# A state-space block and its MLP on one core: token rows as pairs of 64-column matmuls, a table set loaded in another place, and a new order of the front

## The chip, the core and the metric

The kernel runs on one core of a Trainium2 chip. The metric is the device time of one execution in microseconds, the median over three runs. A core has five engines that run side by side and wait for each other by semaphores: PE (TensorE, matrix multiply, with PEld for its weight loads), DVE (VectorE), ACT (ScalarE), POOL (GpSimd) and SP, which here only issues transfers (DMA).

## The reference

The inputs are one sequence of 2048 tokens with 512 channels, in bf16. Two layers follow each other, both with a residual: a long convolution whose kernel is made from a diagonal state-space model (128 states for each channel), and an MLP of width 1376.

```python
dt = exp(log_dt)[:, None]
P = exp((dt * (A_re + 1j * A_im))[:, :, None] * arange(L))
K = einsum("dn,dnl,dn->dl", C, P, dt * B).real          # 512 x 2048
y = irfft(rfft(pad(u)) * rfft(pad(K)))[:L] + u * Dskip   # u = layernorm(x)
h = x + y
h2 = h + gelu(layernorm(layernorm(h)) @ w1 + b1) @ w2 + b2
```

## The kernel before

The convolution is done with a Fourier transform of length 4096 that is split into two stages of matmuls, so that a token number falls into a partition and a row: the view `xv` of the input, `(p j) d -> p j d` with `j` of 16, puts token 16 p + j on partition p as row j.

The front (everything up to the MLP) runs in these stages, which overlap:

- `prefix` makes small constants on POOL and DVE: `bits` and `pf` hold pieces of the partition number, `mask` says which of eight columns belongs to a partition, `cols` and `bw` hold factors and phases.
- `first_stage` makes from them `BD`, the matrix of the first stage of the transform, and `D` (in the profile `Dm`), its transpose, which at the end turns frequencies into token rows. Both have two halves h of 128 columns. In each half a column is zero unless its q, the partition number's last three bits, has the parity h, so half the columns of `D[:, h]` are zero.
- `params` computes the step (`step`, the exponential of `log_dt`), then `th` and the phases `psi`, `psw` and `five`; `exps` computes exponentials of `th` into `Pt` and `Q` on ACT; `p_half` and `q_half` multiply them by sines (`pv`, `qv`, `s`, `sq`); `kgen` makes samples of K with small matmuls (`kps`), writes them to DRAM (`KD`) and reads them back in another layout (`kt`). This is done twice, for channels 0 to 255 (half 0) and 256 to 511 (half 1).
- `norm_in` normalises the tokens (`st`, `rs`, `u`), multiplies them by `BD` (`aps`), and sends the result through DRAM (`A_dram`) into `X`. `x_stage` does the second stage (`xps`).
- `conv` makes the spectrum of K from `kt` (`kfps`, then `kf`), multiplies it with `X` (`pa`, `pb`), transforms back (`zps`, then `z`), and sends z through DRAM (`Zd`) into `ZT`, where the contraction index lies on the partitions. When X has been read, `residual` loads the tokens into it again; its first two calls come in the front, on POOL and SP, the last two in `late_loads`.
- Token rows: `early_rows` (tiles y0, half 0 of rows 0 to 7) and `head_rows` (tile yh, half 1 of rows 0 to 3) add the residual with a matmul by the identity and add `D[:, 0]` and `D[:, 1]` times `ZT` into the same PSUM tile. In the MLP `y_rows` (tile y1, half 1 of rows 4 to 7) and `y_row` (tile y2, a full row of 512) do the same, without the identity. The profile writes y0, y1 and y2 all as y: L1113 and L1115 are those of `half_rows`, L1224 is `y_row`.

The MLP (`mlp`) runs over four blocks of four rows: `up` makes `h1ps` (4 matmuls for each of 11 pieces of the hidden width) with a GELU on ACT, `down` makes `o2ps` (11 matmuls for each row), and DVE adds the residual h and SP writes the row out. `y_row` of the next block stands between the `up` steps of the present one, two matmuls at a time after each second step.

What sets the order: every piece of the front is an `S.op` with a number. The list `ORDER` holds 4 x number + choice, in the order in which the pieces are emitted, and so in which they stand in each engine's queue; the choice picks the engine where a piece may run on either of two. Each engine takes its queue strictly in this order. The dependencies written in `S.op` (such as `x0`, the list of the back transforms, in the calls that make `r0`) are what the search for the order had to keep. The MLP stands in the order of the code.

The activation tables of ACT are loaded when a function of another set comes: the helper `logs` loads the set for logarithm and exponential if the last marked set is not this one, `sines` marks the other. In `step` the exponential of `log_dt` stands without `logs`.

Of the kernel before, what the change touches and what calls it, by code (L numbers as in the profile page):

```python
# [16 lines left out]
P = 128  # L17
# [64 lines left out]
def bc(ap, shape):  # L82
    return ap.to_broadcast(shape)

# [35 lines left out]
def stt(nc, out, a, s, b, o1, o2):  # L120
    nc.vector.scalar_tensor_tensor(out, a, s, b, o1, o2)
# [67 lines left out]
def prefix(nc0, S, K, cp, ct, c2):  # L189
# [41 lines left out]
    split = ((3, 15), (0, 7), (0, 1), (1, 1))  # L231
    bits = c2.tile([P, 4], i32, name="bits")
    for n, (sh, m) in enumerate(split):
        ts(nc, bits[:, n:n + 1], pi[:], sh, ALU.logical_shift_right, m, ALU.bitwise_and)
    pf = ct.tile([P, 4], f32, name="pf")
    nc.vector.tensor_copy(pf[:], bits[:])
    t1, q, odd, b1 = (pf[:, n:n + 1] for n in range(4))
# [9 lines left out]
    t1s = col(t1, 1.0 / 64, 0.0)  # L247
# [12 lines left out]
    ts(nc, mask[:], kf[:, 0:8], q, ALU.is_equal)  # L260
# [222 lines left out]
def params(nc, S, K, cp, pp, sc, cv, psp, raws, ldt, dtb, grb):  # L483
    T, S2, Z = {}, S.op, {}

    def step():
        for h in range(2):
            d = slice(HW * h, HW * h + HW)
            nc.scalar.activation(dtb[:, d].rearrange("p (j g) -> p g j", g=4), ldt[:, d].rearrange("p (g j) -> p g j", g=4), ACT.Exp)
# [530 lines left out]
def head_rows(nc, S, K, psp, cv, o_tail):  # L1020
    K.o_head = []
    for n in range(2):
        cell = {}

        def main(cell=cell, n=n):
            cell["y"] = psp.tile([P, 2, 512], f32, name="yh", tag="p", bufs=PB)
            for r in range(2):
                o, j = cell["y"][:, r, 0:HW], 2 * n + r
                nc.tensor.matmul(o, lhsT=K.ident[:], rhs=K.X[:, j, 1, 0:HW], start=True, stop=False)
                for h in range(2):  # L1030
                    nc.tensor.matmul(o, lhsT=K.D[0:96, h], rhs=K.ZT[0:96, 1, h, j, :], start=False, stop=False)
# [23 lines left out]
        m = S.op("PE", 0.65, main, K.o_z[0:6] + K.o_r0[0:1] + [o_tail], acq="p")  # L1055
# [54 lines left out]
def half_rows(nc, K, out, hh, js, more=False):  # L1110
    for j in range(js.start, js.stop):
        if more:
            nc.tensor.matmul(out[:, j - js.start], lhsT=K.ident[:], rhs=K.X[:, j, hh, 0:HW], start=True, stop=False)  # L1113
        for h in range(2):
            nc.tensor.matmul(out[:, j - js.start], lhsT=K.D[:, h], rhs=K.ZT[:, hh, h, j, :], start=(h == 0 and not more), stop=(h == 1))  # L1115
# [16 lines left out]
def early_rows(nc, S, K, psp, z0, r0):  # L1132
    for n in range(2):
        cell = {}
        js = slice(4 * n, 4 * n + 4)

        def mm(cell=cell, js=js):
            cell["y"] = psp.tile([P, 4, HW], f32, name="y0", tag="p", bufs=PB)
            half_rows(nc, K, cell["y"], 0, js, True)

        def keep(cell=cell, js=js):
            nc.scalar.copy(K.h[:, js, 0:HW], cell["y"][:])

        def stats(cell=cell, js=js):
            for j in range(js.start, js.stop):
                nc.vector.bn_stats(K.st[:, j, 0, :], cell["y"][:, j - js.start])

        m = S.op("PE", 1.35, mm, z0 + r0[n:n + 1], acq="p")
        s = S.op("DVE", 1.5, stats, [m], rel=[m])
        k = S.op("ACT", 1.0, keep, [m], rel=[m])  # L1150
        K.o_early.append(S.op("NONE", 0.0, lambda: None, [s, k]))
# [38 lines left out]
def residual(q, K, xv, n):  # L1190
    q.dma_start(K.X[:, 4 * n:4 * n + 4, :, 0:HW], xv[:, 4 * n:4 * n + 4].rearrange("p j (h d) -> p j h d", h=2))


def mlp(nc, tc, K, w1, w2, b2, xv, ov):
    with tc.tile_pool(name="m_sb", bufs=1) as sb, tc.tile_pool(name="m_rot", bufs=2) as rot, tc.tile_pool(name="m_ps", bufs=2, space=PSUM) as ps1:
# [25 lines left out]
        def y_row(tb, jj):  # L1221
            yp = yps[tb, jj] = ps1.tile([P, 1, 2, HW], f32, name="y2", tag="yps")
            for h in range(2):
                nc.tensor.matmul(yp[:, 0], lhsT=K.D[:, h], rhs=K.ZT[:, :, h, 4 * tb + jj, :], start=(h == 0), stop=(h == 1))  # L1224
# [40 lines left out]
        def down(tb, jj):  # L1265
            j, h = 4 * tb + jj, hT[tb % 2]
            parts = 2 if tb == 3 and jj == 3 else 1
            for n in range(parts):
# [7 lines left out]
                nc.sync.dma_start(ov[j][:, d], ot[:])  # L1276
# [39 lines left out]
def kernel(ctx, tc, A_u, A_A_re, A_A_im, A_B_re, A_B_im, A_C_re, A_C_im, A_log_dt, A_Dskip,  # L1316
# [25 lines left out]
    xv = x_dram.rearrange("(p j) d -> p j d", j=16)  # L1342
# [14 lines left out]
    for n in range(4):  # L1357
        nc.sync.dma_start(x[:, 4 * n:4 * n + 4], xv[:, 4 * n:4 * n + 4])
# [56 lines left out]
    r0 = K.o_r0 = [S.op(("POOL", "SP"), (0.8, 0.45), lambda e, n=n: residual(nc.gpsimd if e == "POOL" else nc.sync, K, xv, n), x0[2 * n:2 * n + 2], lat=3.0) for n in range(2)]  # L1415
# [5 lines left out]
    mlp(nc, tc, K, B_w1, B_w2, B_b2, xv, out_dram.rearrange("(p j) d -> j p d", j=16))  # L1421
# [31 lines left out]
```

## Time and profile before

| what | us |
|---|---|
| three runs | 261.58, 263.01, 263.51 |
| median | 263.01 |
| span of the profiled execution | 260.3 |

The span goes from the first to the last instruction of one profiled execution on its only core; the whole time of that execution isn't listed beside it, so it is told here by the distance from the runs: the shortest is 1.3 above the span, the median 2.7. The transfers move 33.61 MB in all, a mean of 129 GB/s. The granted clock of TensorE was 1.000.

How to read the lines that follow: a row of the timeline has the start and the duration in us, the engine, the line of the code, the operation, output <- inputs, shapes, a count, and in brackets the idle time of the engine just ahead, with what ended it. A row of the chain of waits has start, duration and what. In a row of stretches, the stretch and its length come first, then the busy time of PE, PEld, DVE, ACT and POOL with instruction counts, the clock, and the share and rate of the DMA engines. Matmuls are pipelined: from start to start is what one costs in a stream, its own duration has a tail that lies beside the next. In the slices each digit is a tenth of busy share in a fortieth of the span.

### The profile page before, as it was taken

How to read it: one execution, taken by the hardware profiler on the slowest of the kernel's cores; microseconds unless marked ns; L12 is line 12 of the kernel's file. 1: busy time of each engine (PE TensorE's matmuls, PEld its weight loads, DVE VectorE, ACT ScalarE, POOL GpSimd, SP SyncE). 2: the span in 40 equal slices, each digit the busy share in tenths (PEclk: the TensorE clock that was granted, in tenths of full speed). 3: DMA queues.
4: the chain of work that ended last, by engine and by line, in shares of the span. 5: the costliest groups of instructions: out<-in, count | busy, mean ns of one | idle time of the engine just before them, and what ended most of it. 6: DMA issues, size and time to landing. Idle time of an engine off the chain costs nothing.

```text
span 260.3 us, 4481 instructions
## 1 busy us (share of the span) xinstructions
PE 220.3 (85%) x1585; PEld 138.3 (53%) x1585; DVE 203.3 (78%) x447; ACT 179.5 (69%) x303; POOL 40.0 (15%) x104
## 2 busy tenths in 40 slices
PE   2899308765688797899999999968999999999994
PEld 2323102322276585567988888857744444444443
DVE  6999999998999999999688999975836754761022
ACT  6999999999999999998833565448604703612810
POOL 8922960000003000100560010010000000000000
PEclk9999999999999999999999999999999999999999
DMA  5802951967695910410189678969541033022001
GB/s 166 293 7 34 191 162 61 162 170 244 183 357 148 227 11 24 139 44 0 53 180 267 185 201 242 264 197 240 141 102 59 1 63 101 0 54 80 31 26 54
DMA packets 49442, 33.61 MB, mean 129 GB/s; under 512 B 22154, under 2 KB 47900, under 8 KB 49164
## 3 DMA queue, kind: packets, MB, share of 16 engines
q1 hardware_dynamic: 47676, 28.66, 41.8%
q0 software_dynamic: 1744, 4.68, 7.1%
q8 instruction: 12, 0.20, 0.3%
q14 instruction: 10, 0.08, 0.1%
HBM read 18.65 MB, written 11.26 MB: 115 GB/s over the span
## 4 chain that ended last, share of the span: by engine, by line
PE 43%; DVE 16%; ACT 6%; DMA 6%; issue 2%; POOL 0%; DVEq 0%; POOLq 0%; ACTq 0%
PE o2ps L1273 14%; PE h1ps L1260 12%; PE kfps L930 8%; DVE Pt L79 5%; DMA ZT<-Zd 4%; DVE Q L79 3%; DVE X L79 2%; PE kps L765 2%; ACT Pt L673 2%; DVE pa L79 2%; DVE pb L79 2%; ACT sq L142 2%; DMA Zd<-z 2%; DVE X L91 1%; PE y L1224 1%
## 5 line engine op out<-in xcount | busy, mean ns | idle before, releaser
L1263 ACT ACTIVATE hT<-h1ps,b_sb 128x512 bf16<-128x512 f32 (+3 forms) x55 | 31.9, 604 | 41.9 <-PE h1ps L1260 40.2
L1260 PE MATMUL h1ps<-y2T,wide 128*128 128x512 bf16 (+3 forms) x220 | 40.5, 336 | 0.6 <-DVE ve L75 0.6
L1273 PE MATMUL o2ps<-w_sb,hT 128*128 128x512 bf16 (+3 forms) x187 | 38.7, 366 | 0.0
L930 PE MATMUL kfps<-kt,M 128*128 128x256 bf16 x320 | 37.9, 273 | 0.0
L79 DVE TENSOR_TENSOR ot<-o2ps,h 128x512 bf16<-128x512 f32 (+1 forms) x17 | 11.0, 658 | 30.3 <-PE o2ps L1273 16.9
L930 PEld LDWEIGHTS <-M 128*128 128x128 bf16 x320 | 31.3, 98 | 4.9 <-issue 1.2
L1260 PEld LDWEIGHTS <-wide 128*128 128x128 bf16 (+1 forms) x220 | 21.8, 100 | 17.0 <-issue 0.8
L1273 PEld LDWEIGHTS <-hT 128*128 128x128 bf16 (+1 forms) x187 | 18.3, 98 | 19.7
L79 DVE TENSOR_TENSOR Pt<-s,Pt 128x512 bf16<-128x512 bf16 (+1 forms) x48 | 23.0, 510 | 0.9 <-ACT s L142 0.3
L844 PE MATMUL aps<-u,BD 128*128 128x512 bf16 x32 | 10.2, 407 | 15.2 <-DVE u L839 11.2
L89 ACT CAST z<-zps 128x1024 bf16<-128x1024 f32 (+1 forms) x15 | 14.8, 992 | 10.6 <-PE zps L969 10.6
L673 ACT ACTIVATE Pt<-th 128x256 bf16<-128x256 f32 x64 | 20.7, 401 | 0.0
L142 ACT ACTIVATE sq<-qv 128x1024 bf16<-128x1024 int16 x20 | 20.1, 1077 | 0.0
L142 ACT ACTIVATE s<-pv 128x1024 bf16<-128x1024 int16 x16 | 16.9, 1077 | 0.0
L89 ACT CAST a<-aps 128x1024 bf16<-128x1024 f32 x16 | 15.8, 1053 | 0.5 <-DMA A_dram<-a 0.5
L738 PE MATMUL qv<-RQ,PQ 128*128 128x512 bf16 (+1 forms) x64 | 11.6, 298 | 4.7 <-ACT a L89 1.6
L844 PEld LDWEIGHTS <-BD 128*128 128x128 bf16 x32 | 3.0, 99 | 21.6 <-DVE u L839 14.3
L91 DVE CAST X<-xps 128x1024 bf16<-128x1024 f32 x12 | 14.3, 1219 | 0.0
L79 DVE TENSOR_TENSOR h<-y,X 128x512 f32<-128x512 f32 x10 | 6.9, 686 | 8.6 <-PE y L1224 5.6
L79 DVE TENSOR_TENSOR Q<-sq,Q 128x1024 bf16<-128x1024 bf16 x20 | 13.0, 685 | 0.1
L681 ACT ACTIVATE Q<-th 128x256 bf16<-128x256 f32 x40 | 13.0, 401 | 0.0
L449 POOL DMA_DIRECT2D Dp<-Dd x24 | 11.9, 504 | 7.2 <-DMA Dd<-ds 6.9
(246 smaller groups left out, 446.9 us busy)
## 6 DMA issues: line engine op xcount, KB each, us to landing
A_dram<-a SPq DMA_DIRECT2D x16, 256.0 KB, 2.6
X<-A_dram SPq DMA_DIRECT2D x4, 1024.0 KB, 7.2
Zd<-z SPq DMA_DIRECT2D x15, 256.0 KB, 3.4
x<-in_A_u_dram SPq DMA_DIRECT2D x4, 512.0 KB, 6.9
ZT<-Zd POOLq DMA_DIRECT2D x8, 256.0 KB, 4.1
ZT<-Zd SPq DMA_DIRECT2D x8, 256.0 KB, 3.6
out_dram<-ot SPq DMA_DIRECT2D x15, 128.0 KB, 1.9
X<-in_A_u_dram SPq DMA_DIRECT2D x3, 512.0 KB
```

The costliest lines, as they stand in the source:

```text
L79: (nc.vector if e == "DVE" else nc.gpsimd).tensor_tensor(out, a, b, op)
L89: nc.scalar.copy(out, in_)
L91: nc.vector.tensor_copy(out, in_)
L142: nc.scalar.activation(out, v.bitcast(i16)[..., 0:2 * n:2], ACT.Sin, scale=S2PI / 65536)
L449: nc.gpsimd.dma_start(t[o::128 // cnt], bass.AP(row.tensor, row.offset + 1024 * kh, [[0, cnt], [1, 1024]]))
L673: nc.scalar.activation(K.Pt[:, 1, :, k, :], K.th[:, ds].rearrange("p (e g) -> p e g", g=4), ACT.Exp, scale=float(8 * k))
L681: nc.scalar.activation(K.Q[:, 1, :, m, :], K.th[:, ds].rearrange("p (e g) -> p e g", g=4), ACT.Exp, scale=float(OFFS[m]))
L844: nc.tensor.matmul(ps[:, h, :], lhsT=K.BD[:, h].rearrange("p a b -> p (a b)"), rhs=cell["u"][:], start=True, stop=True)
L930: nc.tensor.matmul(ps[:, k, c, :], lhsT=K.M[:, t, k0 + k, c, :], rhs=kt[:, t, :], start=((plain or c == 1) and t == 0), stop=(t == 4))
L1260: nc.tensor.matmul(pt[:fs, 0:n], lhsT=K.w1_sb[:, dc, fc * P:fc * P + fs], rhs=(y2T[tb][:, dc, js, :] if tb or js.start else K.y2T[:, dc]). ...
L1263: nc.scalar.activation(hT[tb % 2][:fs, fc, cols], pt[:fs, 0:n], ACT.Gelu_apprx_tanh, bias=K.b1_sb[:fs, fc:fc + 1], scale=1.0)
L1273: nc.tensor.matmul(pt[:], lhsT=h[:fs, fc, jj * P:(jj + 1) * P], rhs=K.w2_sb[:fs, fc, d], start=(fc == 0), stop=(fc == NFC - 1))
```

## The change

Three things are changed.

The tokens are dealt in another way: the new view `dealt`, `(p h j) d -> h p j d`, puts token 32 p + 16 h + j on partition 64 h + p as row j. Two pieces of the partition number (`tk`, and `tq` with `th`, a local name that isn't the `th` of `params`) take the place of `t1` and `q` in `bw` and `mask`. With this the columns of `D[:, h]` that aren't zero are those of partitions 64 h to 64 h + 63. So a token row no longer adds two products of 128 columns in one tile: each half h is a matmul of 64 columns that writes its own 64 partitions of the tile. In `half_rows` and `head_rows` all identity matmuls of a tile come first and then all pairs. A residual load covers 64 partitions and 8 rows where it covered 128 and 4, so each early tile waits for both, and both wait for four back transforms.

`step` calls `logs` ahead of its exponentials.

`ORDER` is a new list. Of it the diff shows its first two lines.

```diff
 ORDER = [
-    128, 120, 124, 116, 136, 132, 1864, 320, 0, 4, 16, 20, 24, 60, 68, 72, 28, 76, 80, 64, 84, 88, 92, 96, 140, 100, 104, 8, 208, 420, 108, 112, 492, 12, 356, 144, 352,
+    124, 128, 1864, 120, 136, 132, 60, 320, 0, 4, 20, 16, 24, 64, 92, 100, 68, 116, 72, 28, 76, 80, 84, 88, 96, 8, 140, 352, 420, 104, 208, 108, 112, 492, 12, 356,
...
+def half(h):
+    return slice(64 * h, 64 * h + 64)
+
+def dealt(x):
+    return x.rearrange("(p h j) d -> h p j d", h=2, j=16)
...
-    split = ((3, 15), (0, 7), (0, 1), (1, 1))
+    split = ((3, 15), (0, 7), (0, 1), (1, 1), (2, 15), (0, 3), (6, 1))
...
-    t1, q, odd, b1 = (pf[:, n:n + 1] for n in range(4))
+    t1, q, odd, b1, tk, tq, th = (pf[:, n:n + 1] for n in range(7))
...
-    t1s = col(t1, 1.0 / 64, 0.0)
+    t1s = col(tk, 1.0 / 64, 0.0)
...
-    ts(nc, mask[:], kf[:, 0:8], q, ALU.is_equal)
+    stt(nc, tq, tq, 2.0, th, ALU.mult, ALU.add)
+    ts(nc, mask[:], kf[:, 0:8], tq, ALU.is_equal)
...
     def step():
+        logs(nc)
         for h in range(2):
...
                 nc.tensor.matmul(o, lhsT=K.ident[:], rhs=K.X[:, j, 1, 0:HW], start=True, stop=False)
+            for r in range(2):
+                j = 2 * n + r
                 for h in range(2):
-                    nc.tensor.matmul(o, lhsT=K.D[0:96, h], rhs=K.ZT[0:96, 1, h, j, :], start=False, stop=False)
+                    nc.tensor.matmul(cell["y"][half(h), r, 0:HW], lhsT=K.D[0:96, h, half(h)], rhs=K.ZT[0:96, 1, h, j, :], start=False, stop=False)
...
 def half_rows(nc, K, out, hh, js, more=False):
+    for j in range(js.start, js.stop) if more else ():
+        nc.tensor.matmul(out[:, j - js.start], lhsT=K.ident[:], rhs=K.X[:, j, hh, 0:HW], start=((j - js.start) % 2 == 0), stop=False)
     for j in range(js.start, js.stop):
-        if more:
-            nc.tensor.matmul(out[:, j - js.start], lhsT=K.ident[:], rhs=K.X[:, j, hh, 0:HW], start=True, stop=False)
         for h in range(2):
-            nc.tensor.matmul(out[:, j - js.start], lhsT=K.D[:, h], rhs=K.ZT[:, hh, h, j, :], start=(h == 0 and not more), stop=(h == 1))
+            nc.tensor.matmul(out[half(h), j - js.start], lhsT=K.D[:, h, half(h)], rhs=K.ZT[:, hh, h, j, :], start=not more, stop=not more or j % 2 == 1)
...
 def residual(q, K, xv, n):
-    q.dma_start(K.X[:, 4 * n:4 * n + 4, :, 0:HW], xv[:, 4 * n:4 * n + 4].rearrange("p j (h d) -> p j h d", h=2))
+    h, rows = n % 2, slice(8 * (n // 2), 8 * (n // 2) + 8)
+    q.dma_start(K.X[half(h), rows, :, 0:HW], xv[h, :, rows].rearrange("p j (c d) -> p j c d", c=2))
...
             for h in range(2):
-                nc.tensor.matmul(yp[:, 0], lhsT=K.D[:, h], rhs=K.ZT[:, :, h, 4 * tb + jj, :], start=(h == 0), stop=(h == 1))
+                nc.tensor.matmul(yp[half(h), 0], lhsT=K.D[:, h, half(h)], rhs=K.ZT[:, :, h, 4 * tb + jj, :], start=True, stop=True)
...
-                nc.sync.dma_start(ov[j][:, d], ot[:])
+                nc.sync.dma_start(ov[:, :, j, d], ot[:])
...
-    xv = x_dram.rearrange("(p j) d -> p j d", j=16)
+    xv = dealt(x_dram)
...
-    r0 = K.o_r0 = [S.op(("POOL", "SP"), (0.8, 0.45), lambda e, n=n: residual(nc.gpsimd if e == "POOL" else nc.sync, K, xv, n), x0[2 * n:2 * n + 2], lat=3.0) for n in range(2)]
+    r0 = K.o_r0 = [S.op(("POOL", "SP"), (0.8, 0.45), lambda e, n=n: residual(nc.gpsimd if e == "POOL" else nc.sync, K, xv, n), x0[0:4], lat=3.0) for n in range(2)]
```

Three places show how instructions stand before and after; the lines of the changed program are 10 to 15 higher than those of the profile.

ACT, from its first instruction on (wb is the sine of bw, M<-M the exponentials of `step`, Q and Pt the exponentials of th). Before:

```order
L1346 ACT_TABLE_LOAD
L142 ACTIVATE wb<-bw 128x2x16
L489 ACT_TABLE_LOAD
L489 ACTIVATE M<-M 128x4x64 x2
L129 ACT_TABLE_LOAD
L681 ACTIVATE Q<-th 128x64x4 x4
L673 ACTIVATE Pt<-th 128x64x4 x12
L609 ACTIVATE five<-five 128x512
```

After:

```order
L1361 ACT_TABLE_LOAD
L152 ACTIVATE wb<-bw 128x2x16
L139 ACT_TABLE_LOAD
L501 ACTIVATE M<-M 128x4x64 x2
L685 ACTIVATE Pt<-th 128x64x4 x2
L693 ACTIVATE Q<-th 128x64x4 x4
L685 ACTIVATE Pt<-th 128x64x4 x12
L621 ACTIVATE five<-five 128x512
```

One table load ahead of the exponentials of th is gone.

PE, at the first tile of `early_rows`, behind the last spectrum matmuls of a unit (ident is the identity, Dm the matrix D). Before:

```order
L930 MATMUL kfps<-kt,M 128x256
L1113 LDWEIGHTS ident
L1113 MATMUL y_2248<-X,ident 128x256
L1115 LDWEIGHTS Dm
L1115 MATMUL y_2248<-ZT,Dm 128x256
L1115 LDWEIGHTS Dm
L1115 MATMUL y_2248<-ZT,Dm 128x256
L1113 LDWEIGHTS ident
```

After, from the last of the four identity matmuls on:

```order
L1126 LDWEIGHTS ident
L1126 MATMUL y_2253<-X,ident 128x256
L1129 LDWEIGHTS Dm
L1129 MATMUL y_2253<-ZT,Dm 64x256
L1129 LDWEIGHTS Dm
L1129 MATMUL y_2253<-ZT,Dm 64x256
L1129 LDWEIGHTS Dm
```

The four identity matmuls now stand together, and eight matmuls of 64 columns follow in a row.

POOL's queue from the samples of K on (KD<-samples writes them, kt<-KD reads them back; wide is the tile that the weights of `head_rows` are put into). Before:

```order
L784 DMA KD_65<-samples 128x1x320 x2
L794 DMA kt<-KD_65 128x4x64 x2
L1191 DMA X<-in_A_u_dram 128x8x256
L784 DMA KD_66<-samples 128x1x320
L1005 MEMSET wide 128x4096
L794 DMA kt<-KD_66 128x4x64
L1015 DMA wide<-Ds 4x8x128 x4
L995 DMA ZT<-Zd_67 16x8192 x5
```

After:

```order
L796 DMA KD_65<-samples 128x1x320
L806 DMA kt<-KD_65 128x4x64
L1017 MEMSET wide 128x4096
L1206 DMA X<-in_A_u_dram 64x16x256
L1007 DMA ZT<-Zd_67 16x8192
L806 DMA kt<-KD_66 128x4x64
L1027 DMA wide<-Ds 4x8x128 x4
L1007 DMA ZT<-Zd_67 16x8192 x2
```

The write of KD of half 1 has moved to SP, which now issues all four of them, and the residual load and a ZT read have come between the fill of `wide` and the read of kt.

More of the change, by code (lines that the diff above doesn't have):

```diff
@@ L230, in prefix @@
         at += n
-    split = ((3, 15), (0, 7), (0, 1), (1, 1))
-    bits = c2.tile([P, 4], i32, name="bits")
+    split = ((3, 15), (0, 7), (0, 1), (1, 1), (2, 15), (0, 3), (6, 1))
+    bits = c2.tile([P, 7], i32, name="bits")
     for n, (sh, m) in enumerate(split):
         ts(nc, bits[:, n:n + 1], pi[:], sh, ALU.logical_shift_right, m, ALU.bitwise_and)
-    pf = ct.tile([P, 4], f32, name="pf")
+    pf = ct.tile([P, 7], f32, name="pf")
     nc.vector.tensor_copy(pf[:], bits[:])
-    t1, q, odd, b1 = (pf[:, n:n + 1] for n in range(4))
+    t1, q, odd, b1, tk, tq, th = (pf[:, n:n + 1] for n in range(7))
     cols = ct.tile([P, 5], f32, name="cols")
@@ L1053, in total @@
                 nc.vector.bn_aggr(K.mv0[:, j, :], K.st[:, j].rearrange("p h s -> p (h s)"))
-        m = S.op("PE", 0.65, main, K.o_z[0:6] + K.o_r0[0:1] + [o_tail], acq="p")
+        m = S.op("PE", 0.65, main, K.o_z[0:6] + K.o_r0 + [o_tail], acq="p")
         i = [S.op(("PE", "NONE"), (0.65, 0.0), pause, [m, K.o_zs[5]]) for _ in range(1 + 2 * n)]
@@ L1146, in stats @@
                 nc.vector.bn_stats(K.st[:, j, 0, :], cell["y"][:, j - js.start])
-        m = S.op("PE", 1.35, mm, z0 + r0[n:n + 1], acq="p")
+        m = S.op("PE", 1.35, mm, z0 + r0, acq="p")
         s = S.op("DVE", 1.5, stats, [m], rel=[m])
@@ L1357 @@
     for n in range(4):
-        nc.sync.dma_start(x[:, 4 * n:4 * n + 4], xv[:, 4 * n:4 * n + 4])
+        nc.sync.dma_start(x[:, 4 * n:4 * n + 4], xv[:, :, 4 * n:4 * n + 4])
     nc.sync.dma_start(K.top[1:2, :], A_Dskip.rearrange("(o d) -> o d", o=1))
@@ L1420 @@
     front.close()
-    mlp(nc, tc, K, B_w1, B_w2, B_b2, xv, out_dram.rearrange("(p j) d -> j p d", j=16))
+    mlp(nc, tc, K, B_w1, B_w2, B_b2, xv, dealt(out_dram))
     order.__exit__(None, None, None)
```

45 rows, old and new, of the table ORDER are left out of this document.

## The prediction

> **What bounds the kernel now.** I read the page first, for the busy shares and the slices.
>
> ```profile
> span 260.3 us, 4481 instructions
> PE 220.3 (85%) x1585; PEld 138.3 (53%) x1585; DVE 203.3 (78%) x447; ACT 179.5 (69%) x303; POOL 40.0 (15%) x104
> PE   2899308765688797899999999968999999999994
> ...
> DVE  6999999998999999999688999975836754761022
> ACT  6999999999999999998833565448604703612810
> ```
>
> No engine is the limit all through. In the first half DVE and ACT show nines together, then PE alone. The view of stretches, cut where the slices change, says how tight each part is.
>
> ```profile
> 25.00:125.00 100.00, 72.65 (x660) 46.73 (x659) 97.34 (x184) 98.51 (x171) 15.20 (x29) 1.00 0.55 139
> 125.00:167.00 42.00, 41.75 (x383) 36.90 (x380) 37.07 (x75) 22.78 (x28) 10.09 (x13) 1.00 0.74 198
> 167.00:182.00 15.00, 12.13 (x114) 10.21 (x112) 9.66 (x35) 8.92 (x21) 1.21 (x2) 1.00 0.90 235
> 182.00:254.00 72.00, 72.00 (x356) 34.98 (x355) 35.65 (x90) 26.67 (x42) 0.00 (x0) 1.00 0.24 61
> ```
>
> From 25 to 125 us ACT is busy for 98.51 of 100 us and DVE for 97.34: both bound that part, and a microsecond counts only if both are spared. From 125 to 167 PE is the limit with 41.75 of 42, and from 182 to 254 it never stops. Between them lies a join, which the chain of work that ended last shows:
>
> ```profile
> 165.92 0.44 ACT h L1142
> ...
> 166.82 0.60 ACT z L89
> ...
> 167.44 3.96 DMA Zd<-z
> ...
> 172.50 9.30 DMA ZT<-Zd
> ...
> 181.84 0.61 PE y L1115 x4
> ```
>
> The last z tile goes through DRAM, and the first token rows of the MLP (y, L1115) start when it is back. So what is saved before 167 us reaches the end through the z tile, and PE work in the shadow of those 13 us of transfers is free.
>
> **Base of the sum.** The span is 260.3; the median of the three runs is 263.01, 2.7 more, for what lies around the span. I keep that 2.7 as it is.
>
> **The table load.** Before, the exponentials of `step` load one set and the next ones load another.
>
> ```profile
> 3.79 1.28 ACT L489 ACT_TABLE_LOAD   x1
> 5.08 1.34 ACT L489 ACTIVATE M<-M 128x256 bf16<-128x256 bf16 x2
> 6.44 1.28 ACT L129 ACT_TABLE_LOAD   x1
> 7.74 1.33 ACT L681 ACTIVATE Q<-th 128x256 bf16<-128x256 f32 x4
> ```
>
> The second load, 1.28 us on ACT, goes. But the exponentials behind it read `th`, and that is late next:
>
> ```profile
> 2.09 0.34 DVE L180 TENSOR_SCALAR bits<-pi 128x1 int32<-128x1 int32 x4 [2.09 <-POOL pi L196]
> 2.86 0.15 DVE L180 TENSOR_SCALAR cols<-pf 128x1 f32<-128x1 f32 x1
> ...
> 3.78 0.16 DVE L180 SCALAR_TENSOR_TENSOR fbase<-pf,cols 128x1 f32<-128x1 f32 x1
> ...
> 6.46 0.69 DVE L79 TENSOR_TENSOR th<-tps_are,M 128x512 f32<-128x512 f32 x1
> ```
>
> `th` needs `step` (end 6.42) and its turn on DVE, where the change puts four small instructions ahead: three more `bits` at (0.34 - 0.15) / 3 = 0.063 us each, 0.19, and one scalar_tensor_tensor of 0.16, together 0.35. So `th` runs from 6.81 to 7.50, and ACT starts at 7.50 instead of 7.74: **0.24 us** gained, not 1.28. Ends: 1.28 if `th` were no limit, and a loss of 0.35 if DVE's delay is what carries on. I take 0.24, since ACT is the fuller of the two. The wider `pf` cast (7 for 4 columns) is free in that chain.
>
> **The order searched anew.** It moves work that stays the same. On DVE and ACT nothing else leaves in the first 125 us, so the best it can do is to fill the idle time there, 100 - 98.51 = 1.49 us of ACT, and as much may be lost by a worse fit. Behind 125 us two casts of kf go from DVE to ACT and one z cast the other way; PE is the limit there (0.25 us idle of 42), so that gives nothing. I take 0, with ends of -1.5 and +1.5.
>
> **The matmul pairs.** Before, a token row takes two matmuls of 128 columns, half of whose weights are zero; after, each half is a matmul of 64 columns, and the two can run side by side.
>
> ```profile
> 162.77 0.38 PE L1115 MATMUL y<-ZT,Dm 128*128 128x256 bf16 x2
> ...
> 162.99 0.27 PE L1113 MATMUL y<-X,ident 128*128 128x256 bf16 x1
> ...
> 197.90 0.59 PE L1224 MATMUL y<-ZT,Dm 128*128 128x512 bf16 x2
> 198.33 1.89 PE L1260 MATMUL h1ps<-y2T,wide 128*128 128x512 bf16 x8
> ```
>
> From start to start a matmul of 256 costs (162.99 - 162.77) / 2 = 0.11 us and one of 512 (198.33 - 197.90) / 2 = 0.215. On the path lie 8 rows of the early part (y, both runs ahead of the last z), 4 rows in the first block of the MLP and 8 full rows (L1224). If each pair takes the time of one matmul, (8 + 4) x 0.11 + 8 x 0.215 = 3.04 us are saved. The 4 rows of `head_rows` lie in the shadow of the z transfer and count nothing.
>
> Against it stands the change of shape: two early runs, two in the first block and eight single pairs, 12 runs, each entered and left, 24 changes. The trace has no matmul of 64 columns. Its nearest rows are the matmuls that use one row of the array, beside full ones:
>
> ```profile
> 43.96 0.10 PEld L703 LDWEIGHTS <-PQ 128*128 128x128 bf16 x1 [0.59 <-issue]
> 44.89 0.59 PE L703 MATMUL pv<-RP,PQ 128*128 128x512 bf16 x2 [0.55 <-ACT s L142]
> ...
> 49.54 0.59 PE L844 MATMUL aps<-u,BD 128*128 128x512 bf16 x2 [0.32 <-ACT a L89]
> ...
> 50.06 0.09 PEld L368 LDWEIGHTS <-three 1*128 1x128 bf16 x1 [0.42 <-issue]
> 50.09 0.27 PE L368 MATMUL v<-crow,three 1*128 1x256 bf16 x1
> ```
>
> Between full matmuls the weights come early: those of L703 at 43.96, 0.93 us ahead of their matmul. Before the one-row matmul they come late: the two of L844 have streamed by 49.54 + 2 x 0.215 = 49.97, the load starts at 50.06 and the matmul at 50.09, 0.12 us behind. I take 0.12 us a change, from this row; 24 x 0.12 = 2.88. Ends: nothing, and 0.16, the whole tail of a matmul (0.27 of the row at 162.99, less 0.11). So the pairs come out at 2.88 - 3.04 = **-0.16 us**, between -3.04 (free) and 24 x 0.16 - 3.04 = +0.8 if the pairs do overlap. A full row then pays 0.24 for 0.215; the four-row runs earn 0.44 for 0.24.
>
> [...]
>
> **The other edits.** Dealing the tokens changes which row lands on which partition, with as many rows and bytes in the loads of x and the writes of the result.
>
> ```profile
> 4.01 2.96 SPq L1358 DMA_DIRECT2D x<-in_A_u_dram  x4
> ...
> 17.63 0.69 DVE L826 BATCH_NORM_STATS2 st<-x 128x6 f32<-128x512 bf16 x1
> ...
> x<-in_A_u_dram SPq DMA_DIRECT2D x4, 512.0 KB, 6.9
> ```
>
> The loads of x are issued by 7.0 and take 6.9, so they land at 13.9 and the statistics read them from 17.63: 3.7 us cover an uneven spread. The writes of the result have no cover at the end; as many rows of 1 KB go out, and I take 0. The residual loads now cover 64 partitions and 8 rows; the one on POOL stands behind the fill of `wide`, ahead of a ZT read and the kt read of the second half. What that queue and SP feed:
>
> ```profile
> 126.15 2.23 SPq L784 DMA_DIRECT2D KD<-samples  x3
> 130.43 0.76 POOL L794 DMA_DIRECT2D kt<-KD  x1
> 130.91 1.68 SPq L794 DMA_DIRECT2D kt<-KD  x3
> ...
> 136.77 6.71 PE L930 MATMUL kfps<-kt,M 128*128 128x256 bf16 x60
> ...
> X<-in_A_u_dram POOLq DMA_DIRECT2D x1, 512.0 KB, 5.3
> ...
> kt<-KD SPq DMA_DIRECT2D x7, 64.0 KB, 3.7
> ```
>
> SP issues a fourth KD write (2.23 / 3 = 0.7 us), so its last kt read, now issued at about 132.1 and landed 3.7 later at 135.8, would land at 136.5, still ahead of 136.77: 0, with up to 1 us if the residual, issued just ahead on POOL with its 5.3 us, holds up that queue's kt.
>
> **Sum.** 260.3 - 0.24 + 0 - 0.16 + 0 = 259.9, and 2.7 around it: **262.6 us**.
>
> **The rivals.** *Cheap changes of shape.* If a change costs 0.03 us, as the matmul at 50.09 follows its own load, the pairs give 0.72 - 3.04 = -2.3 and the time is 263.0 - 0.24 - 2.3 = 260.5; with free ones 259.7, and with a front that also fits better 259. For it: the four matmuls of a run share one change. Against: the late load at 50.06.
>
> *The pairs do not overlap* (the change doesn't do what it says). If the second half waits for the first, nothing is saved and each change is paid: 2.88 at 0.12 gives 263.0 - 0.24 + 2.88 = 265.6, and 3.9 at 0.16 gives 266.6. This is slower than before; at 0.12 a change the gain is gone as soon as two halves take 1.13 times one (3.04 x 0.87 = 2.64 = 2.88 - 0.24), and it is 1% slower at 2 times. For it: the trace shows no two matmuls side by side, they start 0.11 or 0.215 apart everywhere. Against: nothing, it is unknown.
>
> *A late kt.* If the kt of the second half holds PE at 136.77 for 1 us, the time is 263.6: within 1%. For it: the margin of 0.3 us above. Against: the fill of `wide` no longer waits for a KD issue.
>
> **How the numbers follow.** The sum as it stands, give or take the front's 1.5: 0.55, with a range of its own of 261.2 to 264.0. Cheap changes 0.25 (259 to 260.8). No overlap 0.12 (265 to 266.6). A late kt 0.08. A measurement of this kernel can tell about 1% from no change, so faster is below 260.4 and slower above 265.6. Faster gets most of the cheap case and the edge of the first, 0.27; slower half of the third and a little of the front's bad end, 0.10; the rest, 0.63, is within 1%. For 8 in 10 the range goes from 259.4 to 265.0.
>
> **What would show it.** The second load at 6.44 gone and the first exponential near 7.5: the first step. Start to start over a full row of the MLP: 0.215 plus twice the price of a change; 0.45 is my sum, 0.28 the cheap case, 0.67 no overlap. PE's wait for kt at the first spectrum of the second half: none. ACT plus DVE idle in 25 to 125: as before. The prediction is wrong if that full row takes under 0.3 or over 0.6, or if the front's end at 125 moves by more than 1.5 us.

## The result and the profile after

The changed kernel takes 297.82 us (median of four runs, 296.46 to 299.52) beside 263.05 for the kernel before (261.58 to 263.51): 1.135 times as long, 95% interval 1.129 to 1.142. The forecast was 262.6. The page of the changed kernel shows at once that PE stands still early on:

```profile
span 297.1 us, 4473 instructions
...
PE   3597000077666879879995999877999999899980
...
PEclk9755555579999999999998899979999999999996
DMA  4111146758767883111067787877921121122111
```

Four slices of PE are at zero from about 30 us on, and from 7 us on the DMA engines show ones: one to two tenths of sixteen engines. The view of stretches gives the numbers (the last three columns are the granted clock, the DMA share and GB/s):

```profile
0.00:25.00 25.00, 16.45 (x62) 6.93 (x63) 19.76 (x62) 20.65 (x40) 12.80 (x60) 0.73 0.23 74
25.00:45.00 20.00, 2.75 (x13) 1.06 (x10) 6.16 (x14) 11.85 (x36) 0.00 (x0) 0.50 0.25 58
```

From 25 to 45 us PE is busy 2.75 of 20 us and DVE 6.16. In the kernel before DVE was busy 19.81 us of that stretch:

```profile
25.00:45.00 20.00, 7.97 (x26) 2.65 (x25) 19.81 (x48) 19.88 (x46) 11.64 (x24) 1.00 0.56 132
```

The timeline of SP's queue and the chain of waits of the changed kernel name the wait:

```profile
4.04 21.12 SPq L1373 DMA_DIRECT2D x<-in_A_u_dram  x4
25.28 9.90 SPq L1374 DMA_DIRECT2D top<-in_A_Dskip_dram  x1
```

```profile
14.45 34.56 DMA x<-in_A_u_dram
49.03 5.44 DVE st L838 x9
...
153.88 7.31 DMA kt<-KD
161.23 8.27 PE kfps L942 x59
...
223.63 7.00 DMA out_dram<-ot
...
282.08 4.78 DMA out_dram<-ot
...
287.70 4.78 DMA out_dram<-ot
```

Four loads of x, which were issued within 3 us and landed 6.9 us later, now keep SP for 21 us, and the last one lands 34.56 us after SP came to it. The statistics end at 54.5 instead of 34.1. At the other end a write of the result takes 4.78 us instead of 1.70, or 7.00 where three of them are issued within 9 us, and the sums on DVE wait for it. The last rows of the statistics and a late write in the kernel before:

```profile
28.05 6.03 DVE L826 BATCH_NORM_STATS2 st<-x 128x6 f32<-128x512 bf16 x10
...
255.19 1.70 DMA out_dram<-ot
```

The group of these sums in the kernel before and in the changed one (after the bar: idle time just ahead, and what ended it):

```profile
L79 DVE TENSOR_TENSOR ot<-o2ps,h 128x512 bf16<-128x512 f32 (+1 forms) x17 | 11.0, 658 | 30.3 <-PE o2ps L1273 16.9 <-DMA out_dram<-ot 13.4
```

```profile
L80 DVE TENSOR_TENSOR ot<-o2ps,h 128x512 bf16<-128x512 f32 (+1 forms) x17 | 11.2, 659 | 43.0 <-DMA out_dram<-ot 30.6 <-PE o2ps L1288 8.2 <-PE h1ps L1275 4.0
```

Both transfers have one thing in common: the view `dealt` gives them a leading dimension of 2. The residual loads, which take one half h of that view, do not have it.

### The profile page after: what moved, and what is told of

Its sections match the earlier page's. It is cut to its first block, busy times and chain, and to the rows that moved or that the text cites. A ratio compares the mean times of both kernels' runs of the same rounds, so it can differ in the third digit from the quotient of the medians.

```text
span 297.1 us, 4473 instructions
## 1 busy us (share of the span) xinstructions
PE 219.6 (74%) x1572; PEld 136.0 (46%) x1585; DVE 203.2 (68%) x450; ACT 178.9 (60%) x303; POOL 36.7 (12%) x99
## 4 chain that ended last, share of the span: by engine, by line
PE 35%; DMA 23%; DVE 19%; ACT 12%; SPq 6%; issue 4%; DVEq 0%; ACTq 0%
DMA x<-in_A_u_dram 12%; PE h1ps L1275 11%; PE o2ps L1288 9%; PE kfps L942 6%; DMA out_dram<-ot 6%; SPq L1373 3%; DVE Pt L80 3%; ACT sq L152 3%; ACT Pt L685 2%; DMA kt<-KD 2%; ACT s L152 2%; PE kps L777 2%; DVE st L838 2%; PE yh L1052 2%; DVE X L101 2%
## 5 line engine op out<-in xcount | busy, mean ns | idle before, releaser
L942 PE MATMUL kfps<-kt,M 128*128 128x256 bf16 x320 | 39.7, 280 | 3.3 <-DMA kt<-KD 3.2
L942 PEld LDWEIGHTS <-M 128*128 128x128 bf16 x320 | 32.1, 100 | 9.4 <-issue 4.9
L856 PE MATMUL aps<-u,BD 128*128 128x512 bf16 x30 | 9.5, 398 | 36.3 <-DVE u L851 32.6
L1275 PEld LDWEIGHTS <-wide 128*128 128x128 bf16 (+1 forms) x220 | 21.0, 100 | 17.6 <-issue 2.5
L838 DVE BATCH_NORM_STATS2 st<-x 128x6 f32<-128x512 bf16 x16 | 10.1, 682 | 20.1 <-DMA x<-in_A_u_dram 20.1
L99 ACT CAST z<-zps 128x1024 bf16<-128x1024 f32 (+1 forms) x14 | 13.5, 988 | 5.0 <-PE zps L981 4.2
```

What stands on the lines that cost most here:

```text
L99: nc.scalar.copy(out, in_)
L838: o = S.op("DVE", 1.1, roots, deps=[S.op("DVE", 0.62, lambda j=j: nc.vector.bn_stats(st[:, j, :], x[:, j, :]), [here[j // 4]]) for j in ra ...
L856: nc.tensor.matmul(ps[:, h, :], lhsT=K.BD[:, h].rearrange("p a b -> p (a b)"), rhs=cell["u"][:], start=True, stop=True)
L942: nc.tensor.matmul(ps[:, k, c, :], lhsT=K.M[:, t, k0 + k, c, :], rhs=kt[:, t, :], start=((plain or c == 1) and t == 0), stop=(t == 4))
L1275: nc.tensor.matmul(pt[:fs, 0:n], lhsT=K.w1_sb[:, dc, fc * P:fc * P + fs], rhs=(y2T[tb][:, dc, js, :] if tb or js.start else K.y2T[:, dc]). ...
```

## The experiments

**What the slow transfers are.** Theory: the leading dimension of 2 lets only 2 of 16 DMA engines work. Two rivals: the dealt rows are slow to reach in any form; or the pairs, the order and the lower clock cost the time. Four kernels tell them apart.

`e1_both_split`, the changed kernel with both transfers written by halves (`e2_x_split` has the first piece alone):

```diff
-        nc.sync.dma_start(x[:, 4 * n:4 * n + 4], xv[:, :, 4 * n:4 * n + 4])
+        h, rows = n % 2, slice(8 * (n // 2), 8 * (n // 2) + 8)
+        nc.sync.dma_start(x[half(h), rows], xv[h, :, rows])
...
-                nc.sync.dma_start(ov[:, :, j, d], ot[:])
+                for c in range(2):
+                    nc.sync.dma_start(ov[c, :, j, d], ot[half(c)])
```

> The changed kernel with the loads of x and the writes of the result each written as one transfer for each half of the partitions (64 partitions outermost, no leading dimension of 2); the same rows go to the same partitions. Theory: a transfer whose view has a leading dimension of 2 is served by 2 of the 16 DMA engines. Then the loads land by about 14 us, the writes take about 2 us, and the time is 260 to 264 us. Rival 1, the dealt rows themselves (which row goes to which partition) are slow to move: 290 or more. Rival 2, the pairs, the new order or the lower clock cost the time: about 297.

Measured: 271.43 us (four runs, 270.37 to 274.22), 1.036 times the kernel before (1.029 to 1.043).

> The changed kernel with only the loads of x mended, the writes of the result as in the change. Theory: the statistics end at about 34 us again instead of 54.5, so some 20 us go and the time is about 277 us, with the writes still at 4.8 to 7 us each and DVE waiting for them. Rival 1 and rival 2: about 297.

Measured: 278.12 us. So the loads of x cost 297.82 - 278.12 = 19.7 us and the writes 278.12 - 271.43 = 6.7. Both rivals fall for these 26.4 us, but the time doesn't return to 260 to 264: some 9 us have another cause.

`e3_deal2` and `e4_deal16` go the other way: the kernel before, with nothing but the dealt view in the two transfers (`e4_deal16` has 16 in place of 2).

```diff
-        nc.sync.dma_start(x[:, 4 * n:4 * n + 4], xv[:, 4 * n:4 * n + 4])
+        nc.sync.dma_start(x[:, 4 * n:4 * n + 4], x_dram.rearrange("(p h j) d -> h p j d", h=2, j=16)[:, :, 4 * n:4 * n + 4])
...
-                nc.sync.dma_start(ov[j][:, d], ot[:])
+                nc.sync.dma_start(ov[:, :, j, d], ot[:])
...
-    mlp(nc, tc, K, B_w1, B_w2, B_b2, xv, out_dram.rearrange("(p j) d -> j p d", j=16))
+    mlp(nc, tc, K, B_w1, B_w2, B_b2, xv, out_dram.rearrange("(p h j) d -> h p j d", h=2, j=16))
```

> The kernel before with nothing but the dealt view, leading dimension of 2, in the loads of x and the writes of the result (so the statistics and the residual rows meet other tokens: the result is that of permuted tokens). Full matmuls, old order, second table load. Theory: about 297 us, all of the loss from two lines. Rival 1: about 297 too. Rival 2: about 263.

Measured: 291.52 us.

> As the last one, but dealt by 16 instead of by 2: the leading dimension is 16, with 8 partitions inside it (the result is again that of permuted tokens). The rows move as far as in the run with 2. Theory: all 16 engines serve it, about 263 us. Rival 1, the permuted rows are slow: 290 or more. Rival 2: about 263.

Measured: 263.27 us, 1.005 times the kernel before (1.001 to 1.010). Rows dealt further apart are not slow; the leading dimension is. Later two more sizes were run:

> The kernel before, dealt by 4 in the loads of x and the writes of the result (the result is that of permuted tokens). Theory, as many engines as the leading dimension has: about 100 GB/s instead of 50 while only x loads, so the 2 MB land by about 26 us, the statistics end 1 to 4 us late and a write takes about 3 us: 265 to 269. Rival, any leading dimension under 16 falls to two engines: about 291.

> As the last one, dealt by 8. Theory: about 200 GB/s, the loads land by about 16 us, ahead of the first statistics, and a write takes about 2.5 us: 263 to 265. Rival: about 291.

Measured: 266.20 with 4, and 263.33 with 8. The view of the transfers from 7 to 40 us, in forty slices, for 2, 4, 8 and 16 in this order (tenths of 16 engines busy; the first slices are those in which only x loads):

```profile
DMA  0111111115111111111111111111111111151111
GB/s 30 50 50 55 55 50 55 55 50 47 35 55 35 35 60 50 60 55 55 50 50 50 55 55 50 50 50 40 60 50 50 50 50 55 55 75 50 50 50 60
```

```profile
DMA  1222222224322222222359229952965998992332
GB/s 79 99 109 99 89 94 99 104 104 106 66 65 90 60 79 104 104 94 94 116 100 223 99 104 104 93 63 43 255 120 136 225 228 177 201 209 60 80 65 55
```

```profile
DMA  4345555475545554542238356999995865277851
GB/s 114 104 139 149 134 134 159 139 145 105 114 114 149 145 80 80 149 145 109 57 45 161 61 108 171 240 254 194 190 192 102 170 119 80 65 179 194 298 224 35
```

```profile
DMA  6898999997200000000037297997799833567400
GB/s 149 223 174 228 268 273 258 248 225 170 41 10 0 10 0 10 0 0 0 6 24 159 54 264 183 202 236 187 157 181 127 170 116 117 204 209 298 169 0 0
```

In the first nine slices (7 to 14.4 us) the digits are 0 and 1 with 2, 1 and 2 with 4, 3 to 5 with 8, and 6 to 9 with 16. That is about what 2, 4, 8 and 16 busy engines of 16 would make (0.125, 0.25, 0.5 and 1). The rates there are 30 to 55 GB/s with 2, 79 to 109 with 4, 104 to 159 with 8 and 149 to 273 with 16. So the four runs fit the theory for these four sizes. The view gives the mean share of the sixteen, not which of them worked, so the number of engines is my estimate from these shares; other sizes of this view weren't run.

**What the other 9 us are.** The first theory was the residual load, which now stands just ahead of the kt reads of the second half on POOL. `e5_resid_behind` moves its entry in `ORDER`:

```diff
-  ..., 2064, 2068, 2460, 2041, ..., 2104, 1877, 1412, ...
+  ..., 2064, 2068, 2041, ..., 2104, 1877, 2460, 1412, ...
```

> The mended kernel (both transfers by halves, 271.4 us) with one entry of the order moved: the residual load on POOL stands behind that queue's kt read and the fills of wide, instead of ahead of them. Theory: the 9 us that are left come from this load, which now needs four steps of the x stage instead of two, is issued at 129.9 us just ahead of the kt reads of the second half, and shares the DMA engines with them (kt 7.3 us instead of 3.8); then PE waits 3.2 us, its clock falls, and the early token rows start 5.5 us late. So about 265 to 267 us, with no wait of PE for kt. Rival, the rest of the new order (a fourth KD write on SP, Zd and ZT rows in other places) makes kt and the join late: about 271. Rival, the pairs: about 271.

Measured: 270.98 us. The wait for kt is gone from the profile (kt lands in 3.1 us instead of 7.3), and the time is the same: this theory falls. What is left of PE's long waits is the one at the first head rows, 3.29 us for ZT. In the same batch ran the order alone, the pairs alone, and the old order with everything else:

> The kernel before with nothing but the new table of the order: full matmuls, undealt rows, second table load. It has the residual load in the late place too. Theory: it carries most of the 9 us, 268 to 272. Rival, the pairs or the dealt rows carry them: 262 to 264.

Measured: 267.58 us, 1.022 times the kernel before (1.015 to 1.030). The order costs 5.7 us with no dealt row and no pair in the kernel. Its profile beside that of the kernel before, on PE:

```profile
138.58 6.60 PE L931 MATMUL kfps<-kt,M 128*128 128x256 bf16 x59 [1.05 <-DMA kt<-KD]
...
171.02 0.58 PE L1032 MATMUL yh<-ZT,Dm 96*128 96x256 bf16 x2 [2.66 <-DMA ZT<-Zd]
...
180.40 5.32 PE L1261 MATMUL h1ps<-y2T,wide 128*128 128x256 bf16 x32 [0.61 <-DVE mv L1054]
```

```profile
166.43 0.38 PE L1031 MATMUL yh<-ZT,Dm 96*128 96x256 bf16 x2
...
174.76 3.65 PE L1260 MATMUL h1ps<-y2T,wide 128*128 128x256 bf16 x32 [0.61 <-DVE ve L75]
```

PE waits for kt and then for ZT, and the MLP's first matmuls start 5.6 us late. These 32 matmuls also take 5.32 us instead of 3.65, at a granted clock of 0.50 from 182 to 184 us. The whole span is 266.4 - 260.3 = 6.1 us longer, so little of that is added to the 5.6.

`e7_full` takes the pairs out of the mended kernel: full matmuls of 128 columns again in all three kinds of token rows, of which the last is shown:

```diff
-                nc.tensor.matmul(yp[half(h), 0], lhsT=K.D[:, h, half(h)], rhs=K.ZT[:, :, h, 4 * tb + jj, :], start=True, stop=True)
+                nc.tensor.matmul(yp[:, 0], lhsT=K.D[:, h], rhs=K.ZT[:, :, h, 4 * tb + jj, :], start=(h == 0), stop=(h == 1))
```

> The mended kernel with full matmuls of 128 columns in all token rows in place of the pairs; rows dealt as in the change, new order. Theory, pairs overlap and a change of shape costs about 0.06 us: a full row takes 0.43 instead of 0.34, so 8 x 0.09 = 0.7 us, 0.2 more in the first block and something for the early rows: 272 to 273. By the forecast's 0.12 a change: within 0.2 of 271.4. If the pairs carry the 9 us: about 263.

Measured: 272.53 us (270.22 to 272.90) beside 271.43: the pairs don't carry the loss. The two ranges overlap, so what the pairs gain isn't told by these times; the traces tell it below.

`e8_old_order` has the old `ORDER` and a residual load that covers four rows again:

```diff
-    h, rows = n % 2, slice(8 * (n // 2), 8 * (n // 2) + 8)
-    q.dma_start(K.X[half(h), rows, :, 0:HW], xv[h, :, rows].rearrange("p j (c d) -> p j c d", c=2))
+    for h in range(2):
+        q.dma_start(K.X[half(h), 4 * n:4 * n + 4, :, 0:HW], xv[h, :, 4 * n:4 * n + 4].rearrange("p j (c d) -> p j c d", c=2))
...
-    ... residual(nc.gpsimd if e == "POOL" else nc.sync, K, xv, n), x0[0:4], lat=3.0) for n in range(2)]
+    ... residual(nc.gpsimd if e == "POOL" else nc.sync, K, xv, n), x0[2 * n:2 * n + 2], lat=3.0) for n in range(2)]
```

> The mended kernel with the old order, and each residual load as two transfers of 64 partitions and 4 rows, so that it needs two steps of the x stage again and stands where it stood before; pairs and the early table load kept. Theory: no wait for kt, 262.2 - 0.24 - 0.9 for the pairs, about 261 (260 to 262.5). Rival, the pairs or the dealt rows carry the 9 us: about 270.

Measured: 263.91 us, 1.008 times the kernel before (1.005 to 1.011): 7.5 us back, but still 2.0 over the kernel before and not 1 under it.

**Which part of the order.** Two hybrids on the kernel before, cut at the first KD write of the second half:

> The kernel before with the new order up to the first KD write of the second half (about 125 us), and everything behind it in the old order. Theory: the 5.7 us that the new order costs by itself arise behind 125 us, where SP waits in ZT reads ahead of Zd writes, ACT waits for a z buffer and PE for ZT and kt; so 261 to 263. Rival, the new front costs them: 266 or more.

> The kernel before with the old order up to the first KD write of the second half, and everything behind it in the new order. Theory: the whole loss of the new order, 266 to 269. Rival, the new front costs it: 261 to 263.

Measured: 263.44 with the new front (1.004, 1.002 to 1.007) and 264.55 with the new back (1.012, 1.006 to 1.017). Both cost something, the back more; 1.2 and 2.3 don't add up to 5.7, but with intervals of 0.6, 1.4 and 2 us either way these runs don't show that the two make each other worse. A second theory for the back was that ten ZT reads on SP's queue stand ahead of Zd writes that are ready. `e12_zt_pool` and `e13_order_mended` change their choice of engine to POOL (each entry plus 1). Both have the residual load behind kt, as in `e5_resid_behind`; the second is without dealt rows and pairs.

> The mended kernel with the residual load behind kt (271.0 us), and the ten ZT reads that the new order puts on SP issued by POOL instead. Theory: SP issues in order, and a ZT read that waits for a Zd write to land holds up the next Zd write, which is ready (2.9 us at one place); the z buffers come free late (ACT waits 3.3 us) and the ZT of the head rows is late (PE waits 3.3 us). Without that 266 to 268. Rival, the z tiles themselves are late by the order of PE, DVE and ACT: about 271.

> The kernel before with the new order in which the residual load stands behind kt and all ZT reads are on POOL; full matmuls, undealt rows. It stands beside 267.6 for the new order as it is. Theory, the queues carry the loss: 263 to 265. Rival, the order of PE, DVE and ACT carries it: 267 or more.

Measured: 270.62 and 270.17 us. This theory falls too; `e13_order_mended` is no faster than the new order as it is. The transfers from 138 to 166 us show what came in place of the waits in the queue, first in `e6_order_only`, then with the ZT reads on POOL in `e13_order_mended` (median us from issue to landing last):

```profile
Zd<-z SPq DMA_DIRECT2D x10, 256.0 KB, 3.4
ZT<-Zd SPq DMA_DIRECT2D x9, 256.0 KB, 3.7
```

```profile
Zd<-z SPq DMA_DIRECT2D x10, 256.0 KB, 7.0
ZT<-Zd POOLq DMA_DIRECT2D x10, 256.0 KB, 6.1
```

With the queue opened, writes and reads are under way together and each takes longer. In `e13_order_mended` PE still waits 2.85 us for ZT, beside 2.66. That the longer transfers use up what the queue gains isn't shown by a run of its own. Which entry of the order costs what stays open.

**The end, and a version that might beat both.** In `e8_old_order` the last sum on DVE waits longer for a write than before, since the tile `ot` has two buffers and the write two pieces back has to land first. The last sum in the kernel before and in `e8_old_order`:

```profile
257.02 0.42 DVE L79 TENSOR_TENSOR ot<-o2ps,h 128x256 bf16<-128x256 f32 x1 [0.91 <-DMA out_dram<-ot]
```

```profile
258.21 0.42 DVE L79 TENSOR_TENSOR ot<-o2ps,h 128x256 bf16<-128x256 f32 x1 [1.77 <-DMA out_dram<-ot]
```

`e9_best`:

```diff
-                ot = rot.tile([P, 512 // parts], bf16, name="ot", tag="ot")
+                ot = rot.tile([P, 512 // parts], bf16, name="ot", tag="ot", bufs=3)
...
-                    nc.sync.dma_start(ov[c, :, j, d], ot[half(c)])
+                    (nc.scalar if c and tb == 3 else nc.sync).dma_start(ov[c, :, j, d], ot[half(c)])
```

> The kernel of the run with the old order (263.9 us; dealt rows, pairs, early table load), with the second half of each result write of the last block issued by ACT instead of SP, and three buffers instead of two for the tile that is written (ot). Theory: the 2.0 us that kernel lost lie at its end, where the last sum waited 1.77 us for the write two pieces back, which SP issued as two transfers (0.47 us more) that took 2.04 us; with a third buffer there is no such wait (0.91 us in the kernel before too). So 261 to 262, at or a little under the kernel before. Rival, the dealt kernel loses elsewhere, in the join where the granted clock fell to 0.50 for 3 us: about 263.

Measured: 262.46 us beside 262.29 (1.001, 0.998 to 1.004). The wait is gone, and the dealt kernel is as fast as the kernel before, not faster. The third buffer alone, in the kernel before:

> The kernel before with three buffers instead of two for the tile of the result (ot), and nothing else. Theory: the last sum no longer waits 0.91 us for the write two pieces back, and the end comes that much earlier: 261.3 to 261.8 beside 262.3, the fastest version here. Rival, the last write then meets the one ahead of it in the DMA engines: 262.3.

Measured: 262.26 beside 262.40 (1.000, 0.998 to 1.003). Its last sum no longer waits for the write, but the runs show no gain of 0.9 us; the theory of a shorter end isn't borne out. Last, the table load alone:

```diff
     def step():
+        logs(nc)
```

> The kernel before with the table set of the logarithm loaded first, and nothing else. By the forecast 0.24 us or less, since the exponentials wait for th: 261.7 to 262.2 beside 262. Rival, the load's whole 1.28 us reach the end: 260.7.

Measured: 262.62 beside 262.29 (1.002, 1.000 to 1.004): no gain, and not 1.28 us. No version here beats the kernel before.

## Why the prediction was wrong, step by step

**The step that failed** stands under "The other edits": "with as many rows and bytes in the loads of x and the writes of the result", then "3.7 us cover an uneven spread" for the loads and "I take 0" for the writes. I counted rows and bytes and never asked how many engines the transfer keeps busy: from 7 to 14 us the mean share of the sixteen is 0.13 in the changed kernel and 0.73 in the kernel before. With a leading dimension of 2, at some 50 GB/s (53 from 7 to 14 us, 50 from 8 to 25), the 2 MB landed 14.45 + 34.56 - 4.04 = 45 us after SP came to the first load, where the statistics of the kernel before read their first row after 17.63 - 4.01 = 13.6 us. The loads cost 19.7 us and the writes 6.7. The step had no rival and no end above zero, so the range couldn't hold the result either.

**The order searched anew** was taken as 0 with ends of 1.5 either way. By itself it costs 5.7 us (267.58 beside 261.91). My bound came from the idle time of ACT in 25 to 125 us; there the idle time of ACT grew by only 0.35 us and that of DVE by 0.65 (`e6_order_only`, ACT busy 98.16 and DVE 96.69 of 100). The larger part of the loss lies behind it, in a part I dismissed because PE was the limit there. A full PE has no idle time to lose to a better order, but a worse one can still give it waits: 1.05 for kt and 2.66 for ZT in `e6_order_only`.

**The late kt**, a rival with a chance of 0.08, came: PE waits 3.2 us for it in the changed kernel, more than the 1 us I allowed, and in `e1_both_split` 3.4. But with the wait taken away (`e5_resid_behind`) the median moved by 0.45 us. The 3.4 us stand in the profile of a run of 274.22 us; how long the wait is in the other runs of `e1_both_split`, from 270.37 us on, isn't shown. The mechanism was seen and it didn't decide.

**The matmul pairs** were sized right, in part by luck: the 0.12 us a change came from a matmul of one row, and the trace before had no pair to test it on. A full row and the run behind it, in the changed kernel:

```profile
227.34 0.41 PE L1239 MATMUL y<-ZT,Dm 128*64 128x512 bf16 x2
227.68 1.90 PE L1275 MATMUL h1ps<-y2T,wide 128*128 128x512 bf16 x8
229.51 0.41 PE L1239 MATMUL y<-ZT,Dm 128*64 128x512 bf16 x2
```

In the kernel before, the start of the next full row, the start of an early run of four rows, and the start of what stands behind that run:

```profile
200.05 0.59 PE L1224 MATMUL y<-ZT,Dm 128*128 128x512 bf16 x2
...
162.66 0.27 PE L1113 MATMUL y<-X,ident 128*128 128x256 bf16 x1
...
163.97 0.27 PE L966 MATMUL zps<-X,R 128*128 128x256 bf16 x1
```

The pair overlaps: 0.34 us from start to start instead of 0.43. But the eight matmuls behind it take 229.51 - 227.68 = 1.83 where they took 200.05 - 198.33 = 1.72. From row to row it is 2.17 us, before it was 200.05 - 197.90 = 2.15. So the pair with both its changes of shape costs 0.34 + 0.11 = 0.45, as the forecast had it, where two full matmuls cost 0.43, and gains nothing. An early run of four rows, here in `e8_old_order`, takes 163.39 - 162.30 = 1.09 us where it took 163.97 - 162.66 = 1.31:

```profile
162.30 0.60 PE L1125 MATMUL y<-X,ident 128*128 128x256 bf16 x4
162.83 0.63 PE L1128 MATMUL y<-ZT,Dm 128*64 128x256 bf16 x8
163.39 0.28 PE L977 MATMUL zps<-X,R 128*128 128x256 bf16 x1
```

That is 0.22 saved beside a forecast of 0.44 - 0.24 = 0.20. A run of two rows in the first block, with the eight matmuls behind it, takes 1.32 us in `e8_old_order` and 1.31 in the kernel before. In all the pairs gain about 2 x 0.22 - 2 x 0.01 - 8 x 0.02 = 0.26 us; the forecast was 0.16. Cheap changes and no overlap, the two rivals, are both out.

**The table load.** The second load is gone and `th` is the next wait, as forecast; the exponentials start at 7.19 instead of 7.74 and not at 7.50, because the four small instructions ahead of `th` on DVE didn't delay it (it starts at 6.46 and takes 0.69 us, as before):

```profile
3.79 1.28 ACT L139 ACT_TABLE_LOAD   x1
5.08 1.35 ACT L501 ACTIVATE M<-M 128x256 bf16<-128x256 bf16 x2
7.19 0.72 ACT L685 ACTIVATE Pt<-th 128x256 bf16<-128x256 f32 x2 [0.76 <-DVE th L80]
```

The term is 0.55 us on ACT instead of 0.24, and by `e11_logs` nothing at the end that can be measured.

**The sum.** The loss is 297.82 - 263.05 = 34.8 us, or 35.9 beside the 261.91 that the kernel before took in the batch of `e6_order_only` and `e8_old_order`. Of these 35.9 us, 26.4 are the two transfers with a leading dimension of 2 (`e1_both_split`, `e2_x_split`). With the old order and residual loads of four rows 7.5 more go (`e8_old_order`); the order alone is 5.7 of them, give or take 2, and the rest, residual loads of half the partitions among it, wasn't told apart. What is then left over the kernel before is 2.0 us, and the profiles, 262.1 beside 260.3, show where 1.8 of it lies: the sum two pieces ahead of the last starts at 254.81 instead of 254.47, 0.34 us late, the last sum waits 1.77 instead of 0.91, and from its end to the end of the span it is 3.47 instead of 2.86. So most of it belongs to the mended writes. In `e9_best`, which changes only the writes, the median is 1.45 us lower, 0.2 over that of the kernel before.

## What to carry to other kernels

Before a changed view is called free, read its outermost dimension: rows and bytes may stay the same while the share of busy DMA engines falls, here from six to nine tenths with an outer dimension of 16 to one tenth with 2. If a layout asks for a small outer dimension, try one transfer for each value of it; here that took 297.82 us to 271.43. And a new order of pieces has no sign before it has run: bound its cost by the waits that a full engine could get, not by the idle time that another one has.

## What the runs showed of the hardware that was not expected

- The slow loads held up the queue that issues them: with a leading dimension of 2 the four loads of x stayed on SP for 21.12 us (2.96 in the kernel before), the small load behind them for 9.90 more (0.30), and the transposes that SP issues next started at 35.78 (23.10).
- The lower granted clock in the changed kernel (0.50 from 25 to 45 us) was not the cause of the loss: in `e3_deal2` the same stretch, with PE busy 3.21 of 20 us, has a clock of 1.00, and DVE's statistics wait as long, 20.8 us beside 20.1. And three of the four runs of the changed kernel have a mean clock of 0.982 to 0.986, beside 0.893 in the profiled one, and still take 296.46 to 299.52 us. Why the clock differs at nearly the same load of PE stays open.
- Short falls of the clock at the join come and go with no change in the work there. In `e8_old_order` it fell to 0.50 while the first 32 matmuls of the MLP ran, 5.32 us instead of 3.65; in `e9_best`, which has the same front, they take 3.65, at a clock of 1.00 from 167 to 187 us. The fall cost next to nothing: PE's first pair of the MLP starts at 182.17 in `e8_old_order` without a wait and at 182.05 in `e9_best` after waiting 1.31 us for ZT. The stretches of `e8_old_order` show clocks of 0.94, 0.50 and 0.71 in three of 2 us each; why the clock fell there and not in `e9_best` isn't shown:

```profile
173.00:175.00 2.00, 1.09 (x10) 0.90 (x11) 1.58 (x9) 0.81 (x2) 0.00 (x0) 0.94 1.07 342
175.00:177.00 2.00, 2.00 (x11) 1.40 (x10) 1.72 (x8) 1.09 (x3) 0.00 (x0) 0.50 1.33 306
177.00:179.00 2.00, 2.00 (x15) 1.58 (x13) 1.08 (x3) 1.25 (x4) 0.00 (x0) 0.71 0.79 134
```
